# A new written order for the work of five engines in a fused scan and mixer kernel

## The chip, the cores and the metric

The kernel runs on one core of a Trainium2 chip. The metric is the time of one execution on the device in microseconds (us), lower is better. The engines are named as the profile names them: PE is TensorE's matmuls and PEld its weight loads, DVE is VectorE, ACT is ScalarE, POOL is GpSimd, SP is SyncE, which here only issues transfers (DMAs).

## The reference

Two blocks in a row. The first is a scan in the manner of Mamba 2 over 4 batches, 8 heads and 768 positions, with 32 channels and a state of 16, done in chunks of 32. The second is a mixer of low rank over the positions, followed by a two-layer network with residuals. The inputs are float32, but U, V and the two weights arrive as float64.

```python
def _attn_ref(x, a, B, C):            # x: (4, 8, 768, 32); a: (4, 8, 768); B, C: (4, 8, 768, 16)
    log_a = np.log(np.clip(a, 1e-06, 1.0))
    for c in range(S // 32):          # chunks of 32 positions
        cum = np.cumsum(la, axis=-1)  # la: log_a of the chunk
        L = np.exp(cum[:, :, :, None] - cum[:, :, None, :]) * causal
        M = np.einsum('bhin,bhjn->bhij', Cc, Bc) * L
        y_intra = np.einsum('bhij,bhjd->bhid', M, xc)
        y_inter = np.einsum('bhin,bhnd->bhid', Cc, state) * np.exp(cum)[:, :, :, None]
        y[:, :, sl] = y_intra + y_inter
        state = decay_full * state + sum_j(Bc * xc * decay_from_j)
...
    x = y as (4, 768, 256)            # positions by heads times channels
    u = x + (x^T @ U @ V)^T           # U: 768 x 32, V: 32 x 768
    out = u + max(u @ w_ch1, 0) @ w_ch2    # w_ch1: 256 x 1024, w_ch2: 1024 x 256
```

## The kernel before

The scan works on pairs of blocks of 128 positions: three pairs in a batch, twelve in all, numbered 0 to 11. The mixer works on a batch at a time: one projection to rank 32, one product back, then three blocks of 256 positions through the two-layer network. The weights arrive as pairs of 32-bit integers (the halves of float64) and are converted on the chip.

The order of all work is written out by hand in `PLANS` (lines 36 to 71) as a list of words, and `follow` executes them one after another. The scheduler is set to manual, so each engine gets its instructions in the order in which the words issue them. An engine never goes past an instruction that waits. A word may issue instructions on several engines, and a word that has several steps appears several times, one step at each appearance. The words that matter here:

- Loads, all on SP's one queue: `B` (B and C of a pair), `X` (x of a pair), `L` (both), `w0` and `w1` (halves of the first quarter of w_ch1, 256 KB each), `w2` to `w4` (its other quarters, 512 KB each), `w5` to `w8` (w_ch2), `Z1` (V) and `Z0` (U). Loads by `B`, `X`, `w` and `L` are held until the last VectorE instruction issued before them is done; `Z` is not.
- Conversion `c`: three steps, with two short VectorE operations and one of ScalarE (L420), one of ScalarE (L422), and three of VectorE. `c0` is U and V, `c1` and `c2` the halves of w1's first quarter, `c3` to `c5` its other quarters, `c6` to `c9` w2. `R` splits a converted quarter in two parts (three operations).
- The scan, with the pair's number behind it, counted from batch 1 (-3 to -1 is batch 0, 0 to 2 batch 1, 3 to 5 batch 2, 6 to 8 batch 3): `Q` or `P` scales B and C (VectorE); `V` or `T` turns them so that positions lie along the free axis (transposes on TensorE, L498, and copies on ScalarE); `D` or `E` decays B; `g` is the product of C and B (L584); `m` and `M` mask its two halves (VectorE); `s` and `u` compute and update the state (L619 on TensorE, then VectorE and POOL or ScalarE); `i` and `j` are the part of the output from the state (L714), `n` the part from within the chunk (L739); `y` copies the output to SBUF (L754 to L761, ScalarE). For the last three pairs `T` goes by four stores into DRAM and one fetch (L526, L532), and its last step scales what was fetched on ScalarE (L551, tile `Cm`).
- The mixer: `O` or `t` brings the output of a pair into another layout; `v` spreads U and V; `p` is the projection (L803) with its copy `pT` on ScalarE (L808); `x` is the product back (L815); `a` adds it to the scan's output (two VectorE operations each, tile `yT`); `U` is a product with w1 in plain float32 (L846) for batch 0's first two blocks; `S`, `f`, `e` and `h` are the same in three parts for all other blocks; `d` is a piece of the product with w2 (L846), whose last pieces add, transpose and store the result. The first number behind `p`, `x`, `a`, `S`, `f`, `e`, `h`, `d`, `U` says which batch: it is counted back from batch 1, so `U1` and `d1` are batch 0, `f0` is batch 1, `f-1` batch 2, `f-2` batch 3.

PSUM has three sets of banks, used in strict rotation: `w` with two, `x` with three, `z` with three. A group that asks for the next bank of a set waits until what was in it has been read.

The instructions of TensorE arrive in blocks of 16 KB by a transfer queue of their own (q8 in the profile): 25 packets in this execution for the whole program.

j-2, named in the prediction, has one small VectorE operation ahead of its products, a copy into the tile `settled`:

```python
    def inter(k, part):
        ...
        if part and "part" not in behind:
            apart(vector.tensor_copy)
        after = behind.pop("part", None)
```

`apart` issues that copy behind the products of the first part (for j-2 in the new order: of i-3), and the products of j wait for it.

Of the kernel before, what the change touches and what calls it, by code (L numbers as in the profile page):

```python
# [36 lines left out]
    0: (  # L37
        'B0 X0 B1 X1 B2 X2 '),
    1: (
        'Z1 F5 A0 Q-3.0 Q-3.1 A1 Q-3.2 F4 V-3.0.0 Q-2.1 V-3.1.5 K2 D-3 g-3 Q-2.2 Q-2.0 V-2.0.2 '  # L40
        'Z0 m-3 M-3 F2 V-2.1.2 Q-1.2 E-1.0 s-3 Q-1.0 D-2 n-3 w0 Q-1.1 V-1.0.2 u-3 F1 V-1.1.3 s-2 '
        'w1 i-3 g-2 u-2 j-3 y-3 F2 g-1 i-2 B3 B4 B5 w2 w3 X3 w4 X4 m-2 M-2 w5 c0 c0 m-1 B6 O-3.0 '
        'c0 M-1 w6 E-1.1 n-2 s-1 u-1 c2 v0 w7 c1 c2 j-2 i-1 y-2 j-1 n-1 c1 y-1 P0 D0 c1 T0 c2 '
        't-2 O-1.3 P2 X5 T0 X6 w8 P1 D2 p1.0.4 p1.4.6 c3 c3 x1 a1.0 a1.1 T1 T2 T2 T1 g0 U1.0.0 '
        'c3 c4 c4 U1.0.1 g1 m0 M0 c5 c4 m1 M1 c5 D1 s0 u0 U1.1.0 U1.1.1 U1.1.2 i0 n0 y0 c6 c6 s1 '
        'c5 g2 c7 u1 R2 m2 c7 U1.1.3 M2 c8 c8 c7 U1.0.2 L4 U1.0.3 i1 n1 y1 c6 R1 R0 c8 R5 c9 s2 '
        'c9 c9 n2 d1.0 L5 R6 u2 R0 d1.1 P3 S1.2 d1.0 R7 d1.0 i2 y2 R3 t1 R1 t0 R2 R5 d1.1 R4 P4 '
        'T3 d1.0 f1.2.0 R4 T4 f1.2.2 t2 e1.2.0 f1.2.1 R6 d1.0 d1.1 D3 R3 h1.2.0 P5 d1.1 e1.2.2 '
        'f1.2.3 e1.2.1 p0 T3 d1.2 e1.2.3 T4 T5 L6 h1.2.2 h1.2.1 R7 d1.1 x0 a0.0 a0.1 d1.2 h1.2.3 '
        'd1.2 d1.2 d1.2 s3 g3 m3 M3 d1.2 d1.2 S0.0 d1.2 g4 m4 M4 d1.2 d1.2 d1.2 d1.2 f0.0.0 '  # L50
        'f0.0.1 e0.0.0 T5 f0.0.2 f0.0.3 d1.2 D4 s4 e0.0.1 u3 e0.0.2 e0.0.3 L7 L8 D5 s5 h0.0.0 i3 '
        'n3 y3 d0.0 d0.0 u4 h0.0.1 g5 h0.0.2 u5 d0.0 d0.0 d0.0 h0.0.3 d0.0 m5 M5 d0.0 P6 d0.0 T6 '
        'n4 S0.1 i4 y4 d0.0 D6 d0.0 d0.0 d0.0 D8 f0.1.2 P7 T7 S0.2 f0.1.3 s6 n5 i5 y5 e0.1.2 '
        'e0.1.3 f0.2.0 u6 t5 h0.1.2 f0.1.0 f0.2.1 f0.2.2 e0.2.0 f0.2.3 e0.2.1 t3 f0.1.1 e0.2.2 '
        'e0.2.3 D7 t4 e0.1.0 h0.1.3 e0.1.1 d0.2 d0.2 d0.2 h0.2.0 h0.2.1 T6 d0.2 t3 h0.2.3 h0.1.0 '
        'd0.1 d0.2 h0.2.2 d0.1 d0.1 d0.1 d0.2 d0.2 d0.2 h0.1.1 d0.1 t4 T7 d0.0 P8 T8 s7 u7 g6 m6 '
        'd0.1 M6 t5 d0.1 d0.2 d0.1 d0.2 d0.2 d0.2 d0.1 d0.1 d0.1 d0.1 s8 u8 n6 i6 y6 p-1 g7 T8 '
        'd0.2 x-1 d0.1 m7 M7 n7 a-1.0 a-1.1 S-1.0 i7 y7 g8 f-1.0.2 f-1.0.3 m8 M8 n8 i8 y8 t6 t7 '
        'S-1.1 e-1.0.2 h-1.0.2 t6 e-1.0.3 f-1.0.0 f-1.0.1 h-1.0.3 t8 f-1.1.3 e-1.0.0 e-1.0.1 '
        'f-1.1.0 h-1.0.0 f-1.1.1 h-1.0.1 d-1.0 S-1.2 d-1.0 f-1.1.2 d-1.0 t7 e-1.1.0 h-1.1.0 '  # L60
        'e-1.1.1 e-1.1.2 e-1.1.3 d-1.1 d-1.0 d-1.0 h-1.1.1 d-1.0 d-1.1 d-1.0 d-1.0 h-1.1.2 d-1.1 '
        'd-1.1 t8 d-1.1 p-2 h-1.1.3 d-1.1 x-2 a-2.0 a-2.1 d-1.1 d-1.1 S-2.0 f-1.2.0 d-1.0 d-1.0 '
        'd-1.1 d-1.0 d-1.0 f-1.2.2 f-1.2.3 f-1.2.1 e-1.2.2 h-1.2.2 e-1.2.3 h-1.2.3 e-1.2.0 d-1.1 '
        'f-2.0.0 h-1.2.0 d-1.1 d-1.1 f-2.0.3 e-1.2.1 h-1.2.1 S-2.1 f-2.0.2 e-2.0.0 f-2.0.1 d-1.2 '
        'e-2.0.2 e-2.0.3 e-2.0.1 h-2.0.2 h-2.0.0 h-2.0.3 f-2.1.1 d-1.0 h-2.0.1 d-1.2 d-1.2 d-1.2 '
        'f-2.1.0 S-2.2 d-1.2 d-1.2 d-1.2 f-2.1.2 d-1.2 f-2.1.3 e-2.1.2 d-1.2 h-2.1.2 d-1.2 d-1.2 '
        'e-2.1.0 e-2.1.1 d-1.2 f-2.2.2 d-1.1 f-2.2.3 e-2.1.3 h-2.1.3 d-2.0 d-2.0 h-2.1.0 d-2.0 '
        'd-2.0 d-2.0 d-2.0 d-2.0 d-2.0 d-2.2 d-1.2 e-2.2.2 h-2.2.2 e-2.2.3 h-2.2.3 f-2.2.0 d-2.0 '
        'd-2.0 d-2.0 f-2.2.1 e-2.2.0 h-2.1.1 d-2.1 h-2.2.0 d-2.1 e-2.2.1 h-2.2.1 d-2.0 d-2.2 '
        'd-2.1 d-2.1 d-2.1 d-2.1 d-2.1 d-2.1 d-2.2 d-2.2 d-2.0 d-2.1 d-2.1 d-2.1 d-2.1 d-2.1 '  # L70
        'd-2.2 d-2.2 d-2.2 d-2.2 d-2.2 d-2.2 d-2.2 d-2.2 d-2.2 d-2.2 '),
}


# [1041 lines left out]
```

## Time and profile before

| what | number |
|---|---|
| time, median of three runs | 214.86 us (214.03 to 215.40) |
| profiled execution, span on the page (the only time that it gives) | 212.4 us |
| TensorE matmuls busy | 202.9 us, 96%, 3190 instructions |
| weight loads busy | 180.9 us, 85% |
| VectorE busy | 173.2 us, 82%, 363 instructions |
| ScalarE busy | 121.0 us, 57% |
| GpSimd busy | 6.3 us, 3% |
| SP's transfers | 20.95 MB, 53.9% of 16 DMA engines' span |
| first product with w1 (U1.0.0) starts | 33.84 us |
| last product with w2 ends | 208.6 us |

The page cuts the span into stretches in which an engine is busy or not; how long an engine stood idle, and what released it, stands in brackets behind a row of the timeline. Matmuls are pipelined, so a row of matmuls counts as busy also where it is not dense. The time of a run includes some us around the profiled span: the median here lies 2.5 us above the span of the one profiled execution.

### The profile page before, as it was taken

How to read it: one execution, taken by the hardware profiler on the slowest of the kernel's cores; microseconds unless marked ns; L12 is line 12 of the kernel's file. 1: busy time of each engine (PE TensorE's matmuls, PEld its weight loads, DVE VectorE, ACT ScalarE, POOL GpSimd, SP SyncE). 2: the span in 40 equal slices, each digit the busy share in tenths (PEclk: the TensorE clock that was granted, in tenths of full speed). 3: DMA queues.
4: the chain of work that ended last, by engine and by line, in shares of the span. 5: the costliest groups of instructions: out<-in, count | busy, mean ns of one | idle time of the engine just before them, and what ended most of it. 6: DMA issues, size and time to landing. Idle time of an engine off the chain costs nothing.

```text
span 212.4 us, 7511 instructions
## 1 busy us (share of the span) xinstructions
PE 202.9 (96%) x3190; PEld 180.9 (85%) x3190; DVE 173.2 (82%) x363; ACT 121.0 (57%) x279; POOL 6.3 (3%) x22
## 2 busy tenths in 40 slices
PE   7988889999999999999999999899999999999994
PEld 5765666878979997988999999589998999999993
DVE  4299979999899999999799995777986299859941
ACT  3354668489969746285588361669713565554310
POOL 4022000000000000000000000000000000000000
PEclk9999999999999999999999999999999999999999
DMA  5997799994751488356755766626510000324354
GB/s 82 138 150 160 89 246 181 190 241 121 102 71 31 79 207 130 88 83 83 108 89 94 149 143 132 112 38 122 117 52 0 0 5 0 49 32 71 49 102 99
DMA packets 120177, 21.43 MB, mean 101 GB/s; under 512 B 110096, under 2 KB 118352, under 8 KB 120144
## 3 DMA queue, kind: packets, MB, share of 16 engines
q1 hardware_dynamic: 120144, 20.95, 53.9%
q8 instruction: 25, 0.41, 0.9%
q14 instruction: 8, 0.07, 0.2%
HBM read 14.39 MB, written 6.55 MB: 99 GB/s over the span
## 4 chain that ended last, share of the span: by engine, by line
PE 75%; DVE 8%; issue 4%; DMA 4%; ACT 3%; SPq 3%; POOL 0%; POOLq 0%; DVEq 0%; ACTq 0%
PE x L846 35%; PE z L846 28%; DMA bc<-in_B_dram 4%; SPq L196 3%; DVE words L170 2%; PE x L584 2%; PE z L739 1%; PE w L803 1%; PE x L714 1%; PE x L739 1%; DVE S L170 1%; ACT yT L759 1%; PE x L815 1%; DVE o L170 1%; DVE BC L170 1%
## 5 line engine op out<-in xcount | busy, mean ns | idle before, releaser
L170 DVE SCALAR_TENSOR_TENSOR words<-words 128x512 fp32r<-128x512 f32 (+6 forms) x60 | 39.4, 669 | 2.4 <-ACT words L420 0.8
L846 PE MATMUL x<-words,w 128*128 128x256 f32 x288 | 38.1, 280 | 0.0
L846 PEld LDWEIGHTS x<-words,w 128*128 128x128 f32 x288 | 34.9, 188 | 1.6 <-issue 1.2
L846 PE MATMUL x<-u,w 128*128 128x256 f32 x240 | 34.3, 282 | 0.0
L846 PE MATMUL z<-u,w 128*128 128x256 f32 x240 | 32.7, 278 | 0.0
L851 ACT ACTIVATE x<-x 128x512 f32<-128x512 f32 (+1 forms) x27 | 15.5, 577 | 28.2 <-PE x L846 26.4
L846 PEld LDWEIGHTS x<-u,w 128*128 128x128 f32 x240 | 30.3, 188 | 0.6 <-ACT yT L759 0.2
L846 PEld LDWEIGHTS z<-u,w 128*128 128x128 f32 x240 | 29.7, 188 | 0.1
L851 ACT ACTIVATE z<-z 128x512 f32<-128x512 f32 (+1 forms) x24 | 13.7, 574 | 12.3 <-PE z L846 10.2
L846 PE MATMUL z<-words,w 128*128 128x256 f32 x144 | 19.6, 280 | 0.0
L846 PEld LDWEIGHTS z<-words,w 128*128 128x128 f32 x144 | 17.7, 188 | 0.9 <-issue 0.9
L170 DVE SCALAR_TENSOR_TENSOR words<-x,words 128x512 fp32r<-128x512 f32 x20 | 13.6, 682 | 4.5 <-ACT words L886 4.4
L170 DVE SCALAR_TENSOR_TENSOR words<-z,words 128x512 fp32r<-128x512 f32 x20 | 13.6, 682 | 2.2 <-ACT words L886 2.2
L886 ACT ACTIVATE words<-x 128x512 fp32r<-128x512 f32 x20 | 12.0, 598 | 3.3 <-PE x L846 3.2
L170 DVE TENSOR_TENSOR yT<-x,yT 128x384 f32<-128x384 f32 (+1 forms) x15 | 9.2, 613 | 5.1 <-PE x L846 2.7
L170 DVE TENSOR_TENSOR BC<-bc,F 128x512 f32<-128x512 f32 (+2 forms) x18 | 8.7, 508 | 5.4 <-DMA bc<-in_B_dram 3.0
L886 ACT ACTIVATE words<-z 128x512 fp32r<-128x512 f32 x20 | 11.8, 597 | 1.7 <-PE x L846 1.2
L170 DVE SCALAR_TENSOR_TENSOR S<-S,kept,w 128x64 f32<-128x64 f32 x40 | 11.2, 279 | 1.7
L584 PE MATMUL x<-Cm,T 32*64 32x128 f32 x192 | 11.6, 307 | 0.6 <-DVE Cm L170 0.4
L651 ACT ACTIVATE Sm<-S,slot 128x128 f32<-128x128 f32 (+1 forms) x18 | 6.0, 385 | 9.9 <-DVE S L170 9.9
L584 PE MATMUL z<-Cm,T 32*64 32x128 f32 x192 | 10.5, 307 | 0.0
L170 DVE TENSOR_TENSOR M<-x,causal 128x256 int32<-128x256 int32 x24 | 9.1, 421 | 1.6 <-PE z L584 1.6
(152 smaller groups left out, 363.5 us busy)
## 6 DMA issues: line engine op xcount, KB each, us to landing
words<-in_moe_w_ch_dram SPq DMA_DIRECT2D x7, 512.0 KB, 5.5
squares<-w1f SPq DMA_DIRECT2D x52, 64.0 KB, 1.9
x<-in_x_dram SPq DMA_DIRECT2D x24, 128.0 KB, 4.1
out_dram<-o SPq DMA_DIRECT2D x32, 64.0 KB, 2.3
bc<-in_B_dram SPq DMA_DIRECT2D x24, 64.0 KB, 3.5
bc<-in_C_dram SPq DMA_DIRECT2D x12, 128.0 KB, 3.9
T<-squares SPq DMA_DIRECT2D x6, 256.0 KB, 4.3
ytok<-squares SPq DMA_DIRECT2D x6, 256.0 KB, 3.6
```

What stands on the lines that cost most here:

```text
L170: self.last = call(*args, **kwargs)
L196: op = nc.sync.dma_start(**kwargs)
L584: nc.tensor.matmul(out=g[r][cols, c], lhsT=s["T"][rows, 0, c, cols], rhs=s["Cm"][rows, :, :, ts(2 * c + p, Q)].rearrange("r v t i -> r v i ...
L651: nc.scalar.activation(s["Sm"][:, sl, v], s["S"][:, sl, ts(v, D)], AF.Copy, scale=slot[:, v, None])
L714: product = nc.tensor.matmul(out=y[r // 2][p][ts(v, H), c], lhsT=own[ts(r, Q)], rhs=s["T"][ts(r, Q), 1, :, ts(2 * c + p, Q)].rearrange("r ...
L739: product = nc.tensor.matmul(out=y[n][p][ts(v, Q), c], lhsT=x_sb[k][half, c, h], rhs=s["M"][half, h // 2, c, h % 2], start=fresh(k, n, p, ...
L759: nc.scalar.copy(out=yp[ts(1 - v, H), n, :, p], in_=y[n][p][ts(v, H)])
L803: nc.tensor.matmul(out=p[ts(n, H)], lhsT=UU[:, c].rearrange("p t r -> p (t r)"), rhs=ytok[b][:, c, ts(n, P)], start=(c == 0), stop=(c == N ...
L815: nc.tensor.matmul(out=h[q][:, :VS], lhsT=pT[rows], rhs=V4[rows], start=True, stop=True, skip_group_check=True)
L846: nc.tensor.matmul(out=t, lhsT=lhsT, rhs=rhs, start=start, stop=True, skip_group_check=True)
L851: nc.scalar.activation(t, t, AF.Copy, scale=1.0 + EPS)
L886: nc.scalar.activation(gs[j, i][0], t, AF.Relu, scale=NEAR)
```

## The change

Only the second plan, `PLANS[1]`, changes (lines 40 to 71). It contains the same words, each as often as before (one `j-2`, three `c3`, and so on), in a new order; the fills `F` are the same. So each engine executes as many instructions of each kind as before. Below are the stretches of which the prediction speaks; the order between them is new as well.

```diff
-        'Z1 F5 A0 Q-3.0 Q-3.1 A1 Q-3.2 F4 V-3.0.0 Q-2.1 V-3.1.5 K2 D-3 g-3 Q-2.2 Q-2.0 V-2.0.2 '
-        'Z0 m-3 M-3 F2 V-2.1.2 Q-1.2 E-1.0 s-3 Q-1.0 D-2 n-3 w0 Q-1.1 V-1.0.2 u-3 F1 V-1.1.3 s-2 '
-        'w1 i-3 g-2 u-2 j-3 y-3 F2 g-1 i-2 B3 B4 B5 w2 w3 X3 w4 X4 m-2 M-2 w5 c0 c0 m-1 B6 O-3.0 '
-        'c0 M-1 w6 E-1.1 n-2 s-1 u-1 c2 v0 w7 c1 c2 j-2 i-1 y-2 j-1 n-1 c1 y-1 P0 D0 c1 T0 c2 '
-        't-2 O-1.3 P2 X5 T0 X6 w8 P1 D2 p1.0.4 p1.4.6 c3 c3 x1 a1.0 a1.1 T1 T2 T2 T1 g0 U1.0.0 '
-        'c3 c4 c4 U1.0.1 g1 m0 M0 c5 c4 m1 M1 c5 D1 s0 u0 U1.1.0 U1.1.1 U1.1.2 i0 n0 y0 c6 c6 s1 '
-        'c5 g2 c7 u1 R2 m2 c7 U1.1.3 M2 c8 c8 c7 U1.0.2 L4 U1.0.3 i1 n1 y1 c6 R1 R0 c8 R5 c9 s2 '
-        'c9 c9 n2 d1.0 L5 R6 u2 R0 d1.1 P3 S1.2 d1.0 R7 d1.0 i2 y2 R3 t1 R1 t0 R2 R5 d1.1 R4 P4 '
...
-        'n3 y3 d0.0 d0.0 u4 h0.0.1 g5 h0.0.2 u5 d0.0 d0.0 d0.0 h0.0.3 d0.0 m5 M5 d0.0 P6 d0.0 T6 '
-        'n4 S0.1 i4 y4 d0.0 D6 d0.0 d0.0 d0.0 D8 f0.1.2 P7 T7 S0.2 f0.1.3 s6 n5 i5 y5 e0.1.2 '
...
-        'd0.1 d0.2 h0.2.2 d0.1 d0.1 d0.1 d0.2 d0.2 d0.2 h0.1.1 d0.1 t4 T7 d0.0 P8 T8 s7 u7 g6 m6 '
-        'd0.1 M6 t5 d0.1 d0.2 d0.1 d0.2 d0.2 d0.2 d0.1 d0.1 d0.1 d0.1 s8 u8 n6 i6 y6 p-1 g7 T8 '
-        'd0.2 x-1 d0.1 m7 M7 n7 a-1.0 a-1.1 S-1.0 i7 y7 g8 f-1.0.2 f-1.0.3 m8 M8 n8 i8 y8 t6 t7 '
...
-        'd-1.1 t8 d-1.1 p-2 h-1.1.3 d-1.1 x-2 a-2.0 a-2.1 d-1.1 d-1.1 S-2.0 f-1.2.0 d-1.0 d-1.0 '
...
+        'F5 A0 A1 Q-3.0 Q-3.1 Q-3.2 F4 V-3.0.0 w0 V-3.1.5 Z1 K2 Z0 g-3 D-3 Q-2.1 s-3 Q-2.2 Q-2.0 m-3 '
+        'M-3 D-2 V-2.0.2 u-3 F2 V-2.1.2 Q-1.2 w3 w1 g-2 s-2 Q-1.0 Q-1.1 V-1.0.2 B4 m-2 u-2 c1 c1 F1 '
+        'V-1.1.3 w2 n-3 M-2 i-2 n-2 E-1.0 c1 i-3 j-2 c0 B3 j-3 c0 c0 E-1.1 c4 w7 X3 c2 s-1 y-3 y-2 '
+        'F2 g-1 u-1 w4 v0 c2 m-1 t-2 M-1 c4 B5 w6 i-1 O-3.0 j-1 P1 n-1 c4 p1.0.4 y-1 c3 O-1.3 c2 '
+        'p1.4.6 w5 c3 P0 T1 X4 x1 T1 a1.0 a1.1 c3 T0 D0 T0 U1.0.0 c8 c5 c5 U1.1.0 w8 B6 g0 m0 R1 c5 '
+        'R2 M0 s0 U1.1.1 c8 U1.1.2 u0 U1.0.1 c7 c8 X5 P2 U1.1.3 c6 g1 m1 c7 L4 c6 R3 U1.0.2 D1 M1 L5 '
+        'T2 T2 c6 U1.0.3 R6 c7 i0 n0 D3 s1 y0 R4 g2 X6 d1.0 u1 m2 d1.1 i1 n1 M2 c9 R5 D2 c9 c9 P4 s2 '
+        'L6 R0 u2 d1.1 d1.1 n2 i2 y1 d1.0 R1 P3 y2 R0 T3 R2 T4 d1.0 S1.2 t0 f1.2.2 R6 f1.2.1 f1.2.0 '
...
+        'T6 D7 n3 y3 d0.0 d0.0 d0.0 d0.0 n4 i4 y4 u5 L8 d0.0 d0.0 g5 m5 S0.2 d0.0 d0.0 f0.1.0 f0.1.1 '
+        'e0.1.0 M5 n5 s6 i5 P7 y5 e0.1.1 T7 f0.1.2 h0.1.0 t5 t3 f0.2.0 e0.1.2 f0.1.3 h0.1.1 f0.2.1 '
...
+        's7 t4 m6 d0.0 d0.2 d0.2 D8 d0.1 d0.1 M6 d0.2 d0.1 u7 g7 s8 u8 d0.1 d0.2 d0.2 d0.2 m7 M7 T8 '
+        'd0.1 d0.2 n6 p-1 d0.2 i6 x-1 a-1.0 n7 i7 a-1.1 y6 S-1.0 g8 y7 t6 f-1.0.2 f-1.0.1 m8 M8 t7 '
...
+        'h-1.1.1 d-1.0 d-1.0 d-1.0 t8 p-2 d-1.0 x-2 h-1.1.0 a-2.0 d-1.0 d-1.0 S-1.2 d-1.0 f-1.2.0 '
...
```

What can be read from it in words: the first half of w1 is loaded ahead of V and U, and the conversion of that half (`c1`) comes ahead of that of U and V (`c0`). The gram and state products of the first pairs follow one another more closely. `i-3` comes behind `n-2`, and `j-2` ahead of `j-3`. All three steps of `c4` and the first of `c3` come ahead of `O-1.3`, which feeds the last projection of batch 0. `P2`, `T2` and `g0` come behind the first products with w1, and these go through the second block (`U1.1.0`) before the second quarter of w1 (`U1.0.1`). Near the start of batch 2's mixer, `p-1` stands ahead of `i6` and `y6` instead of behind them, `g7` stands far ahead of `n6`, and the last step of `T8` (Cm on ScalarE) stands ahead of `p-1`. `p-2` has a piece of a down product between it and `x-2`.

36 rows, old and new, of the table PLANS are left out of this document.

## The prediction

> **What bounds the kernel now.** I read the busy shares first, then busy time by stage, then the timelines where TensorE (PE) is not full.
>
> ```profile
> PE 202.9 (96%) x3190; PEld 180.9 (85%) x3190; DVE 173.2 (82%) x363; ACT 121.0 (57%) x279; POOL 6.3 (3%) x22
> ...
> q8 instruction: 25, 0.41, 0.9%
> ```
>
> TensorE is busy for 202.9 of 212.4 us and the change takes no instruction away, so only its 9.5 us of gaps, the part of the start in which matmuls wait while counted as busy, and the tail can change. By stage (length, then busy us and instructions of PE, weight loads, DVE, ACT and POOL, granted clock, DMA share, GB/s):
>
> ```profile
> 0.00:34.00 34.00, 29.22 (x627) 21.63 (x628) 24.92 (x79) 18.16 (x48) 6.27 (x22) 1.00 0.86 147
> 34.00:60.00 26.00, 25.37 (x486) 20.64 (x487) 24.34 (x58) 19.25 (x44) 0.00 (x0) 1.00 0.74 155
> 60.00:100.00 40.00, 39.78 (x564) 35.22 (x564) 38.90 (x76) 26.84 (x62) 0.00 (x0) 1.00 0.59 101
> ...
> 130.00:140.00 10.00, 9.29 (x313) 6.78 (x313) 8.09 (x19) 5.39 (x18) 0.00 (x0) 1.00 0.60 116
> 140.00:160.00 20.00, 20.00 (x269) 19.16 (x267) 15.64 (x28) 11.93 (x26) 0.00 (x0) 1.00 0.38 81
> 160.00:200.00 40.00, 40.00 (x354) 39.45 (x354) 30.39 (x49) 20.79 (x38) 0.00 (x0) 1.00 0.17 27
> ```
>
> The clock is 1.00 throughout, so it is no term. From 140 to 200 TensorE is gapless: a delay put in before 140 reaches the end in full unless a later wait absorbs it. From 34 to 100 VectorE (DVE) is nearly as full (63.2 of 66 us), so what is moved on it shifts all behind it. The places that can move are the start up to the first up product (U1.0.0, 33.84), the waits of 34 to 60, two spots near 96, and 130 to 140.
>
> **The change part by part.** Every engine has the same instructions; only their order differs. The sum starts from the profiled execution's span, 212.4; the page gives no other time of its own, and the median, 214.86, lies 2.5 above the span. I add the 2.5 at the end.
>
> *Loads.* The 256 KB half of w1 that comes first goes ahead of V and U on SP, whose earlier loads are issued back to back until 13.05. Such a load landed 4.6 us after its issue, so 17.7; its conversion c1 now stands where VectorE arrives at about 17.8. The other weight loads also come before their conversions, with 512 KB landing after 5.5. Value 0, between 0 and 0.8 (if the 5.5 holds for the first half too).
>
> *Instruction blocks.* TensorE stops inside a word where nothing releases it:
>
> ```profile
> 20.87 0.18 PEld L739 LDWEIGHTS x<-M,x 64*32 64x32 f32 x6
> 21.60 0.10 PEld L739 LDWEIGHTS x<-M,x 64*32 64x32 f32 x1 [0.55 <-issue]
> ```
>
> Stops fall at every 256th PE instruction where the 256 before were short ones: 0.38 lost at 16.78, 0.66 at 21.60, 0.38 at 25.53, 0.43 at 96.42 (inside n3): 1.9 in all. The new order gives n3's block 5.1 us of dense work ahead of its end instead of 3.1, which ends that stop, and leaves 3.24 us in the block that ends in i4, which should start one. Value 0; between -1.9 (all stops gone) and +1.5 (three more like the mean). The Trainium skill, page "Runtime: NRT & Kernel Launch", section "Instruction fetch mechanics", says that the sequencer fetches the next block of 256 instructions while it executes the current one, and calls a crossing mostly hidden. By that the four stops would be near zero before and after, and the term 0 with no chance of -1.9; the 0.55 above is against it for short instructions, while the stretch 140 to 200 is for it.
>
> *The start, on VectorE.* The rows:
>
> ```profile
> 29.84 1.29 DVE L170 TENSOR_TENSOR BC<-bc,F 128x512 f32<-128x512 f32 x2 [1.36 <-DMA bc<-in_B_dram]
> ...
> 32.06 0.55 DVE L170 TENSOR_TENSOR yT<-x,yT 128x384 f32<-128x384 f32 x1
> ...
> 33.45 0.55 DVE L170 TENSOR_TENSOR yT<-z,yT 128x384 f32<-128x384 f32 x1
> ```
>
> The yT rows are a1.0 and a1.1; a1.0 releases U1.0.0. Adding the rows of every word ahead of a1.0, VectorE has 26.76 us of work before it now and 28.10 then: +1.34 (c4's first and last steps, 0.88 and 2.14, come forward; D0 0.42, D2 0.42, P2 0.69 and small others go back). P2's wait of 1.36 leaves the path, because P2 moves behind U1.1.2: -1.36. Q-2.1 no longer fills the wait at 9.95: +0.3. The new wait is j-2's small copy (0.14), which must follow TensorE's i-3, itself now behind n-2 and M-2; queued behind it on VectorE are c0, c4, u-1, m-1 and M-1, and so n-1, y-1, the last projection of batch 0 and x1. The nearest row is the same copy for j-3, which waited nothing at 17.40; the other bound is i-3 plus its dependants, 1.5. In the new order M-2 comes right ahead of n-2, n-2 and i-3 last 0.9 and 0.5 on TensorE, and VectorE has c1's last step of 1.26 in between, which covers a part: I take +0.85, nearer to the second row. Sum +1.13, so a1.0 starts at 33.2 at the overlap that VectorE's rows show now, and at 33.9 if the moved work runs without it; 33.5 taken. a1.0's two operations last 1.02: U1.0.0 at 34.55, +0.7 (0.4 to 1.1).
>
> *TensorE's work ahead of U1.0.0.*
>
> ```profile
> 31.19 1.09 PE L498 MATMUL w<-ident,BC 128*128 128x128 f32 x8 [0.22 <-DVE BC L170]
> ...
> 33.84 1.99 PE L846 MATMUL x<-yT,w1f 128*128 128x256 f32 x8
> ```
>
> Now the turns of pair 2 (two, 0.49 each) and g0 (0.86) run while TensorE would wait for a1.0; in the new order both come behind U1.0.0, so the cover is gone and 1.84 us more work lies behind it: +1.84. If they fitted later gaps it would be 0; by 60 only 1.6 us of gaps are there, below. Together with the start: +2.5.
>
> *34 to 60.* A late TensorE finds some results ready. U1.0.1 lost 0.42 waiting for c3; c3's last step is 1.34 us of VectorE work later, but U1.1.0, 1.8 us, now stands ahead of U1.0.1. The plain down product lost 0.6 (0.43 to 0.75) waiting for c9; VectorE's work ahead of c9's last step is 54.59 against 54.33, so it is as early as it was. Both go: -1.0. The 0.6 near 46.6, for y0's copies ahead of the next x and z banks, stays: g2 and d1.0 now stand behind y0. +1.5 by 60.
>
> *60 to 130.* x0's two groups follow M3 more closely: +0.2. n3's saved 0.43 is in the block term, and 0.7 more is saved where i3, s5 and d0.0 waited; against that g5 waits for banks that y4 empties, with two down products (0.9) over y4's copies of 0.27 (+0.4), and n5, e0.1.2 and f0.2.0 stand closer to M5 and y5 (+0.7): net +0.4, between -0.7 (cover holds everywhere) and +1.4 (no cover for y4).
>
> *130 to 140.* ScalarE is in the way now:
>
> ```profile
> 133.13 0.27 ACT L761 COPY yT<-x 128x128 f32<-128x128 f32 x1 [0.63 <-DVE o L170]
> ...
> 134.68 0.27 ACT L808 COPY pT<-w 128x128 f32<-128x128 f32 x1
> 135.31 0.91 ACT L551 ACTIVATE Cm<-T,slot 128x256 f32<-128x256 f32 x2 [0.36 <-DMA T<-squares]
> ```
>
> pT stands behind y6's six copies, and x-1 follows at 135.00; TensorE lost 2.3 us from 130 to 142. Afterwards pT comes ahead of y6, and g7 is earlier (-2.3), but n6 now waits for the banks that M7 reads (one mask step, 0.7), x-1 (0.3), n7 (0.4) and g8 (0.6) for copies and masks put closer to them: +2.0; net -0.3. p-2 gets a down product behind it that hides its copy: -0.3 of 0.45. The tail is left as it is: the last product ends 3.8 before the end in both, as its chain (add, transpose, four stores) is the same.
>
> The sum: 0 + 0 + 0.7 + 1.84 - 1.0 + 0.2 + 0.4 - 0.3 - 0.3 = +1.5; 213.9 of span, and with 2.5, 216.4.
>
> **The rivals.**
> *Slower, by the Cm of pair 8 on ScalarE (L551).* In the new order its two operations, which wait for a fetch by DMA, stand ahead of pT's copy (now they are behind it). Behind them on ScalarE wait pT, then y6, y7 and the scalings of the first products; x-1, a-1.0 and S-1.0 wait for pT, and all of batch 2's mixer for those. A fetch landed 4.3 us after its issue (131.02 to 135.3). SP's queue puts it behind t4's fetch and the four stores of a finished block (4.8 us for seven such issues now), so it can be issued near 130 at the earliest: landing 134.3, Cm done 135.2, as pT is wanted at about 135. From an issue at 131 on, each us goes to the end in full. At 133, where SP's stores stood in the profile (132.47), it is +2, and with 0.7 for TensorE's next bank +2.7: 216.4 + 2.7 = 219.1. For it: L551 waited for that DMA (0.36) even now, with six copies ahead of it. Against: 130 would be on time.
> *Faster, because the early delay is not handed on.* j-2 finds i-3 done (-0.85), the two turns and g0 fit gaps that I counted as lost (-1.84), and the block stops go (-1.9); the two waits of 34 to 60 then come back in full (+1.0): 213.9 - 3.6 = 210.3 of span, 212.8; with the -0.7 bound of 60 to 130 in place of +0.4, 211.7. Centre 212.3. For it: P2's 1.36 is really removed, and no other wait at the start is longer but that of Q-2.1. Against: VectorE has 1.34 us more ahead of a1.0.
> *No effect.* The start is late by 1 to 2 us and the waits at 46.6, 96 and 135 absorb it, as they are waits for engines that did not get later: 214.9.
>
> **How the numbers follow.** My forecast has 0.36, the slower rival 0.26, the faster 0.28, no effect 0.10. The time is the likeliest's, 216.4. One per cent, 2.15 us, is about what can be told from no change here: faster is below 212.7, slower above 217.0. Of the faster rival's cases, 211.7 to 212.8 and up, 0.20 of its 0.28 lie below 212.7. Slower takes the 0.26 and 0.11 of my forecast, the cases with the loads' 0.8 or the blocks' +1.5: 0.37. Within 1%: 0.43. The range goes from 211.7, the faster rival's low end, to 220.0, the slower rival with one more us of late fetch; the forecast alone is 214.8 (j-2's wait and the +0.7 of 60 to 130 gone) to 218.7 (loads and blocks at their upper ends).
>
> **What would show it right or wrong.** Right: U1.0.0 starts at 34.3 to 35.2, with one turn of pair 2 and L584's g0 behind it; DVE shows a wait ahead of the settled copy and none for in_B_dram near 30; TensorE shows no idle time for w1f or o words in 34 to 60; an issue stop moves from 96 to the block in i4; ScalarE's pT row lies ahead of yT's in the stretch near 135. The slower rival shows as L551 waiting over 1 us for T right ahead of L808. Wrong: U1.0.0 before 33.8, no stops at all in the early blocks, or a gap of over 1 us in 140 to 200, of which I foresee none.

## The result: 1.2% slower

The changed kernel takes 217.92 us (median of seven runs, 216.91 to 219.23) against 215.65 (214.03 to 216.17): a ratio of 1.0123, 95% interval 1.0085 to 1.0161. On a second chip the unedited new order came to 1.0181 (1.0124 to 1.0237). Its profiled execution spans 215.1 us, of a run of 217.2, beside the 212.4 of the profile before. The forecast was 216.4. The direction was right; several of its terms were not.

First the page of the changed kernel: busy time, and the granted clock in 40 slices of 5.4 us.

```profile
PE 204.1 (95%) x3190; PEld 181.3 (84%) x3190; DVE 173.1 (80%) x363; ACT 122.7 (57%) x279; POOL 6.3 (3%) x22
...
PEclk9997589999999999999999999999999999999999
```

Then the same stretches as before (length, busy us of PE, weight loads, DVE, ACT, POOL, clock, DMA share, GB/s):

```profile
0.00:34.00 34.00, 26.83 (x566) 19.51 (x566) 22.39 (x72) 15.46 (x41) 6.34 (x22) 0.85 0.91 161
34.00:60.00 26.00, 25.93 (x397) 20.44 (x404) 25.35 (x61) 21.51 (x47) 0.00 (x0) 1.00 0.78 139
60.00:100.00 40.00, 40.00 (x625) 36.02 (x630) 37.44 (x72) 25.74 (x60) 0.00 (x0) 1.00 0.42 81
...
130.00:140.00 10.00, 10.00 (x302) 8.21 (x300) 7.51 (x20) 5.19 (x15) 0.00 (x0) 1.00 0.52 101
140.00:160.00 20.00, 19.66 (x284) 17.73 (x283) 16.18 (x30) 13.11 (x31) 0.00 (x0) 1.00 0.47 93
160.00:200.00 40.00, 40.00 (x352) 39.83 (x351) 28.49 (x46) 20.98 (x37) 0.00 (x0) 1.00 0.19 34
```

The start is where it differs: 61 TensorE instructions fewer by 34 us, VectorE busy 2.5 us less (22.39 against 24.92), and a clock of 0.85 where before had 1.00. From 34 to 60 TensorE is fuller than before. So VectorE did not have too much to do at the start, as the prediction had it: it waited.

VectorE's timeline of the changed kernel shows for what:

```profile
18.37 0.56 DVE L169 TENSOR_SCALAR words<-words 128x256 int32<-128x256 int32 x2 [1.20 <-DMA words<-in_moe_w_ch_dram]
18.86 0.59 DVE L169 TENSOR_SCALAR Cm<-x,slot 128x128 f32<-128x128 f32 x2
19.38 0.74 DVE L169 TENSOR_TENSOR M<-z,causal 128x256 int32<-128x256 int32 x2
...
22.40 0.15 DVE L169 COPY settled<-slot 128x1 f32<-128x1 f32 x1 [1.16 <-PE z L713]
...
33.87 0.42 DVE L169 COPY ytok<-z 128x256 f32<-128x256 f32 x1 [1.33 <-PE z L768]
```

The first row is c1, waiting for w0. It was issued at 14.25, not at 13.05, and landed 4.1 us later. Behind it on VectorE stand V-1.1.3's copy (Cm) and the mask M-2, and TensorE's i-2 needs a bank that M-2 reads:

```profile
17.11 0.35 PE L713 MATMUL x<-T,Sm 32*64 32x64 f32 x4
19.93 0.37 PE L713 MATMUL z<-T,Sm 32*64 32x64 f32 x2 [2.46 <-DVE M L169]
```

From there to x1 the chain that ended last in the changed kernel runs nearly without a break through TensorE's short words, and then through ScalarE. A part of it (start, us, what):

```profile
24.50 1.15 PE x L139 x2
...
27.56 0.74 PE z L1011 x8
28.30 0.52 ACT V L1015 x2
28.82 0.41 ACT words L421
29.23 0.55 ACT ytok L782
29.78 0.62 ACT words L421
30.40 0.48 ACT ytok L782
30.88 0.04 issue
30.93 0.28 PE z L713 x2
```

L139 is the idle fill F2 ahead of g-1, L1011 is v0. The last L782 is O-3.0's copy, for which j-1's products wait (the role that a `settled` copy has elsewhere): on ScalarE it stands behind v0's two copies, c2, t-2 and c4. So x1 starts at 35.15 instead of 30.04 and U1.0.0 at 36.72 instead of 33.84.

How much of that reaches the end is read from TensorE's lateness: the start of a word less the unhindered lengths of all TensorE words ahead of it in that kernel's own order (0.91 for an f, 0.45 for an e or d, 0.25 for a T, which is two transposes, and so on, as they last in the dense stretches of before; where words run a little shorter than that, it falls). From the two profiles:

| at | before | after | difference |
|---|---|---|---|
| x1 | 4.02 | 9.38 | +5.4 |
| U1.0.0 (after: T2 and g0 still to come) | 5.12 | 9.35 | +4.2 |
| d1.0 | 5.14 | 8.73 | +3.6 |
| x0 | 3.58 | 6.73 | +3.2 |
| s8 | 6.49 | 9.25 | +2.8 |
| f-1.0.2 | 8.46 | 10.55 | +2.1 |
| last product | 9.79 | 12.54 | +2.75 |

The two spans differ by 2.7: the account closes. The start loses 5.4, later stages give back 3.3 of it (their waits are for engines that did not get later), and the tail loses 0.7.

One execution is not a rule, though. Three executions with before's start had U1.0.0 at 33.84, 34.20 and 35.32; three with the new start at 36.72, 36.79 and 38.26. The shown profile of before is the earliest of its kind, and the difference of the means is 2.8. It is also the only one of the fourteen profiles in which the granted clock stays at 1.00 from the start to the end of the products. So the table is the account of this pair, not of every pair.

### The profile page after: what moved, and what is told of

It is laid out like the page before. It is cut to its first block, busy times and chain, and to the rows that moved or that the text cites. A ratio compares the mean times of both kernels' runs of the same rounds, so it can differ in the third digit from the quotient of the medians.

```text
span 215.1 us, 7532 instructions
## 1 busy us (share of the span) xinstructions
PE 204.1 (95%) x3190; PEld 181.3 (84%) x3190; DVE 173.1 (80%) x363; ACT 122.7 (57%) x279; POOL 6.3 (3%) x22
## 4 chain that ended last, share of the span: by engine, by line
PE 86%; SPq 6%; ACT 3%; DMA 2%; DVE 1%; issue 1%; ACTq 0%
PE x L845 37%; PE z L845 28%; SPq L195 6%; PE x L583 3%; PE x L738 2%; PE w L802 2%; PE z L738 2%; DMA words<-in_moe_w_ch_dram 2%; PE w L618 2%; PE z L713 2%; PE x L713 2%; PE x L814 2%; PE x L802 1%; PE w L497 1%; PE z L583 1%
## 5 line engine op out<-in xcount | busy, mean ns | idle before, releaser
L845 PE MATMUL x<-words,w 128*128 128x256 f32 x288 | 40.7, 282 | 0.0
L845 PEld LDWEIGHTS x<-words,w 128*128 128x128 f32 x288 | 35.9, 188 | 1.9 <-issue 1.4
L845 PE MATMUL x<-u,w 128*128 128x256 f32 x240 | 33.8, 281 | 0.5 <-ACT x L850 0.5
L845 PE MATMUL z<-u,w 128*128 128x256 f32 x240 | 33.1, 278 | 0.0
L845 PEld LDWEIGHTS x<-u,w 128*128 128x128 f32 x240 | 30.0, 188 | 1.3 <-ACT x L850 0.9
L845 PEld LDWEIGHTS z<-u,w 128*128 128x128 f32 x240 | 29.8, 188 | 0.2
L845 PE MATMUL z<-words,w 128*128 128x256 f32 x144 | 19.9, 277 | 0.0
L845 PEld LDWEIGHTS z<-words,w 128*128 128x128 f32 x144 | 17.9, 188 | 0.1
L713 PE MATMUL z<-T,Sm 32*64 32x64 f32 x180 | 8.5, 254 | 3.5 <-DVE M L169 2.5
L583 PE MATMUL x<-Cm,T 32*64 32x128 f32 x192 | 10.5, 317 | 1.4 <-ACT Cm L507 1.0
L169 DVE TENSOR_TENSOR BC<-bc,F 128x512 f32<-128x512 f32 (+2 forms) x18 | 9.2, 531 | 1.7 <-ACT F L371 1.5
L169 DVE TENSOR_TENSOR u<-yT,u 128x512 fp32r<-128x512 f32 x10 | 6.9, 687 | 4.3 <-ACT u L839 4.3
L583 PEld LDWEIGHTS x<-Cm,T 32*64 32x64 f32 x192 | 6.6, 138 | 4.2 <-ACT Cm L507 1.2
```

Of the source, the lines that this page charges most:

```text
L169: self.last = call(*args, **kwargs)
L583: nc.tensor.matmul(out=g[r][cols, c], lhsT=s["T"][rows, 0, c, cols], rhs=s["Cm"][rows, :, :, ts(2 * c + p, Q)].rearrange("r v t i -> r v i ...
L713: product = nc.tensor.matmul(out=y[r // 2][p][ts(v, H), c], lhsT=own[ts(r, Q)], rhs=s["T"][ts(r, Q), 1, :, ts(2 * c + p, Q)].rearrange("r ...
L845: nc.tensor.matmul(out=t, lhsT=lhsT, rhs=rhs, start=start, stop=True, skip_group_check=True)
```

## The experiments

All are edits of the written order. Ratios are to before on the same chip. One row each, with U1.0.0 from its profile:

| run | U1.0.0, us | ratio (95% interval) |
|---|---|---|
| changed kernel | 36.72 | 1.0123 (1.0085 to 1.0161) |
| after_again | 38.26 | 1.0181 (1.0124 to 1.0237) |
| m2_before_c1 | 36.02 | 1.0115 (1.0052 to 1.0178) |
| fill_the_gap | 36.99 | 1.0092 (1.0058 to 1.0126) |
| ytok_early | 36.60 | 1.0058 (1.0019 to 1.0098) |
| m2_and_ytok | 37.45 | 1.0051 (1.0008 to 1.0094) |
| m2_and_no_fill | 34.78 | 1.0095 (1.0063 to 1.0127) |
| after_to_85_then_before | 36.79 | 1.0069 (1.0031 to 1.0108) |
| before_to_85_then_after | 34.20 | 1.0068 (1.0025 to 1.0111) |
| before_to_88_then_after | 35.32 | 1.0060 (1.0018 to 1.0101) |
| before_to_25_then_after | 42.24 | 1.0336 (1.0275 to 1.0396) |
| before_t2_g0_late | 34.28 | 0.9964 (0.9924 to 1.0004) |
| before_no_fill | 34.69 | 0.9947 (0.9908 to 0.9986) |

**The wait for w0.**

```diff
- m-2 u-2 c1 c1 F1 V-1.1.3 w2 n-3 M-2 i-2
+ m-2 u-2 F1 V-1.1.3 w2 n-3 M-2 c1 c1 i-2
```

> The changed kernel, with the first two steps of c1 moved behind M-2, so that the mask M-2 and V-1.1.3's copy no longer stand on VectorE behind the wait for w0's load. Theory W (the start is late because of this one wait: VectorE idle 1.20 us, TensorE idle 2.6 us, and then a granted clock of 0.5 from 18.7 to 28.6 us): the clock is 1.00 throughout, TensorE's gap before i-2 is under 0.5 us, U1.0.0 starts at 34 to 35 instead of 36.72, and the time is 2 to 3 us under the changed kernel, 215.0 to 216.0. Rival V (VectorE's order decides: it has more work ahead of a1.0, and the wait only hides that): U1.0.0 at 36 or later, time within 0.7 us of the changed kernel, 217.2 to 218.6.

The gap ahead of i-2 shrank as meant (from 2.46 to 0.71 us), and n-2 started 1.2 us sooner (19.36 instead of 20.55), but U1.0.0 only 0.7, and the ratio did not move. The granted clock fell all the same, to 0.5 from 18.3 to 28.6. The weight loads of this run show that other waits remained:

```profile
18.71 0.21 PEld L713 LDWEIGHTS z<-T,Sm 32*64 32x64 f32 x2 [0.83 <-POOL Sm L646]
...
22.06 0.18 PEld L713 LDWEIGHTS z<-T,Sm 32*64 32x64 f32 x2 [0.33 <-issue]
...
30.22 0.14 PEld L713 LDWEIGHTS z<-T,Sm 32*64 32x64 f32 x2 [0.93 <-ACT ytok L782]
```

The stop at 22.06, inside j-2, comes 1.3 us after a packet of instructions had landed (19.80 to 20.76), and j-1 still waits for O-3.0's copy. Theory W, that the one wait makes the loss, is refuted: neither its clock nor its start nor its time came. The wait is one link; the 0.7 us are less than the 1.5 by which two executions of the unedited order differ (the control, below). Rival V's numbers all but came (36.02; 218.63), but its reason is not shown by that: what j-1 waits for here is ScalarE.

**The clock.** In the new order it is at half for 10.2 us, as the stretches show (columns as above):

```profile
16.00:18.00 2.00, 1.46 (x72) 1.05 (x70) 1.00 (x4) 0.30 (x2) 0.75 (x2) 1.00 0.95 252
18.00:20.00 2.00, 0.07 (x4) 0.10 (x6) 1.63 (x6) 1.36 (x4) 0.58 (x2) 0.67 0.99 326
20.00:22.00 2.00, 2.00 (x86) 1.71 (x88) 1.20 (x4) 0.37 (x1) 0.00 (x0) 0.50 1.04 198
22.00:28.00 6.00, 5.74 (x114) 3.54 (x106) 5.04 (x17) 2.98 (x8) 0.51 (x1) 0.50 0.74 137
28.00:30.00 2.00, 2.00 (x28) 1.48 (x24) 1.67 (x4) 1.72 (x5) 0.00 (x0) 0.77 0.88 170
```

Two runs ask what that costs. One fills the gap:

```diff
- V-1.1.3 w2 n-3 M-2 i-2 n-2
+ V-1.1.3 w2 n-3 M-2 F6 i-2 n-2
```

> The changed kernel, with three more idle products of TensorE (F6: about 2.1 us of work whose results nobody reads) put in front of i-2, into the gap in which TensorE waits for M-2; the wait itself stays. It parts the clock from the wait. Theory W1 (a gap of over 1.3 us costs the clock, and the clock at half is a cost of its own): the granted clock stays 1.00 in 18 to 29 us, i-2 still starts near 19.9, U1.0.0 comes 1 to 2 us sooner than 36.72, and the time is 216.2 to 217.2. Rival W2 (the clock at half lies under VectorE's work and costs nothing): clock 1.00, but U1.0.0 at 36.5 or later and a time of 217.5 to 218.3.

The clock stayed at 1.00 until 22, then fell for two windows anyway, and U1.0.0 did not come sooner (36.99). So neither theory's condition, a clock of 1.00 to 29 us, was met, and the run does not part them. At 23.16 this run has a stop of 0.87 for instructions, 1.3 us after a packet that landed at 21.83. The other run takes the fills out of before, which leaves TensorE less busy:

```diff
- F2 V-2.1.2    F1 V-1.1.3    F2 g-1
+ V-2.1.2       V-1.1.3       g-1
```

> The kernel before without its three idle fills F2, F1 and F2 (TensorE products that nobody reads, some 0.7, 0.4 and 0.7 us, ahead of V-2.1.2, V-1.1.3 and g-1). It asks what the clock is worth at the start in an order that has no wait for w0. Theory C (half clock on a chain of TensorE's own work costs time): the granted clock falls to 0.5 in one to three windows of 3.4 us between 15 and 29, U1.0.0 comes 0.5 to 2 us later, the ratio 1.003 to 1.010. Rival W2 (half clock lies under VectorE's work): the clock falls, U1.0.0 stays within 0.4 us and the ratio within 0.997 to 1.003.

```profile
14.00:18.00 4.00, 2.25 (x85) 1.50 (x74) 3.54 (x13) 1.93 (x7) 1.20 (x2) 1.00 0.89 199
18.00:22.00 4.00, 3.82 (x97) 3.33 (x97) 2.82 (x11) 1.71 (x4) 0.97 (x2) 0.56 0.68 124
22.00:26.00 4.00, 4.00 (x128) 2.89 (x127) 3.64 (x11) 1.59 (x5) 0.51 (x1) 0.59 0.82 93
```

The clock fell to half here as well, and the kernel got faster: 215.24 against 216.68 us, ratio 0.9947 (0.9908 to 0.9986). Theory C's ratio is refuted for the old order, and W2 falls short on the good side: the fills cost more than what they keep. That rests on the ratio alone: U1.0.0, at 34.69, came 0.85 later than in the profile of before, which is C's number, though inside the scatter of the old start (33.84 to 35.32), and this profile has a stop for instructions of 1.59 us at 48.72 that the one of before has not. By the ratio this version beats both kernels.

What half clock costs in the new order, whose chain runs through TensorE's own words from 20 to 28, stays open: in no run was the clock full with all else alike. The executions of before beside these experiments give a hint for the old order (79 of them, each against the mean on its own chip). With a clock of 1.00 over the whole execution (34 of them) they took 0.27 us less than that mean; with about 0.99, which is one window of 3.4 us at half (37), 0.16 more; with less (8), 0.40 more. So one window goes with 0.4 us, give or take 0.2; whether it is the cause is not shown. The changed kernel's executions list 0.974 to 0.984, two or three windows; if each cost as much there, an estimate from these numbers, some 1 us of the 2.65 would be the clock's.

**ScalarE's queue ahead of j-1.**

```diff
- y-2 F2 g-1 ... i-1 O-3.0 j-1
+ y-2 O-3.0 F2 g-1 ... i-1 j-1
```

> The changed kernel with O-3.0 (the turned output of pair 0, whose copy on ScalarE the products of j-1 wait for) moved from behind i-1 to ahead of g-1; j-1 then waits for a small VectorE copy behind i-1 instead. Theory S (the start is late because j-1 waits on ScalarE, whose queue holds v0's two copies, c2, t-2's copy and c4 ahead of O-3.0's copy: chain 26.74 to 30.93 in the new profile): j-1 starts at 29.6 to 29.9 instead of 30.93, U1.0.0 at 35.4 to 36.0 instead of 36.72, and the time is about 1 us under the changed kernel, if later waits do not take it back. Rival C (the granted clock of 0.5 from 18.7 to 28.6 us decides the start): U1.0.0 stays at 36.4 or later.

j-1 started at 30.65 instead of 30.93, and U1.0.0 at 36.60. The edit put in a wait of its own, since O-3.0 needs y-3's copies, and g-1 now queues behind it:

```profile
24.82 0.72 PEld L768 LDWEIGHTS x<-ident,yT 128*128 128x128 f32 x4 [0.69 <-ACT yT L753]
```

Theory S's numbers did not come. Rival C's did (36.4 or later), but the new wait ahead of g-1 would give the same, so the clock is not shown to be the cause. The ratio, 1.0058, is below the 1.0181 of the same kernel unedited, measured on another chip; nothing in its profile explains that, so it isn't counted as a gain.

With both edits together:

> Both edits of the start: c1 behind M-2, and O-3.0 ahead of g-1. Theory S with the wait for w0 as its first half: M-2's 1.2 us are no longer swallowed by ScalarE's queue, so j-1 starts at 28.5 to 29.0, U1.0.0 at 34.2 to 35.2, the time 215.0 to 216.5 beside a before of 215.5 to 217, about level with it. Rival C: clock 0.5 in two or three windows of 3.4 us from 18 us on, U1.0.0 at 35.8 or later, a time above before's by 1% as the changed kernel's.

n-2 was the earliest yet (19.05), and j-2 then stopped for 1.58 us inside itself:

```profile
22.63 0.14 PEld L713 LDWEIGHTS z<-T,Sm 32*64 32x64 f32 x2 [1.58 <-issue]
```

The packet with those instructions landed at 21.37. Theory S's numbers did not come (j-1 at 31.49); U1.0.0, at 37.45, is where rival C had it, its 1% is not: what the two edits gained was lost to the block of instructions and to O-3.0's wait. The ratio of 1.0051 with such a profile again can't be put down to a cause.

**Taking work off the chain.** m2_before_c1's edit, and the new order's three fills left out:

> The changed kernel with c1 behind M-2, and without the three idle fills F2, F1 and F2 ahead of V-2.1.2, V-1.1.3 and g-1. In the new profile the last fill lies on the chain (24.50 to 25.65, 1.15 us at half clock), between s-1 and g-1, where nothing waits on VectorE. Theory K (the start of the new order is one chain through TensorE, M-2's wait and then the queue of short words behind it, so that each piece taken off it shows): x1 at 32.8 to 34.0 instead of 35.15 (36.69 in the second profile), U1.0.0 at 34.4 to 35.6, the ratio to before 1.002 to 1.010 against 1.012 and 1.018 of the unedited order. Rival B (the blocks of instructions and ScalarE's copies end at the same time as the chain, so that nothing shows): x1 at 34.5 or later, the ratio above 1.010, as in m2_before_c1.

x1 at 33.22 and U1.0.0 at 34.78 are where theory K put them, and the last product ends earliest of all runs with the new start; the ratio, 1.0095, is at the upper edge of K's range. This was the only edit of the new start that moved U1.0.0 by more than 1 us from the first profile's 36.72. It is one execution, though, and the fastest of its eleven (216.01, with a median of 217.80); the ratio hardly differs from that of m2_before_c1 (1.0115). So theory K fits the profile, and a gain in time is not shown. What is left of the waits in it:

```profile
22.41 0.18 PEld L713 LDWEIGHTS x<-T,Sm 32*64 32x64 f32 x2 [1.17 <-issue]
...
28.99 0.13 PEld L713 LDWEIGHTS z<-T,Sm 32*64 32x64 f32 x2 [1.31 <-ACT ytok L782]
```

**Pair 2's turn (T2, T2) and g0 by themselves.** The prediction's largest term, put into before:

```diff
- x1 a1.0 a1.1 T1 T2 T2 T1 g0 U1.0.0 c3
+ x1 a1.0 a1.1 T1 T1 U1.0.0 T2 T2 g0 c3
```

> The kernel before with one edit: the turns of pair 2 and g0 come right behind U1.0.0 instead of ahead of it. This is the prediction's +1.84 by itself. By the prediction: U1.0.0 starts up to 0.7 us sooner, 1.84 us of TensorE's work comes later, so +1.1 us at U1.0.1 less what its wait for c3 (0.42) gives back: +0.7 at 41 us, and +0.5 to +1.1 at the end. Rival: TensorE only waits less further on, and the time is within 0.3 us of before's.

0.9964 (0.9924 to 1.0004): no loss, against the +0.5 to +1.1 us of the prediction. U1.0.0, with less ahead of it, waits for a1.0 instead, and U1.0.1's wait for c3 is still there, at 37.60:

```profile
34.28 0.30 PEld L845 LDWEIGHTS x<-yT,w1f 128*128 128x128 f32 x2 [1.06 <-DVE yT L169]
...
37.60 1.59 PEld L845 LDWEIGHTS z<-yT,w1f 128*128 128x128 f32 x8 [0.43 <-DVE w1f L169]
```

It is the ratio that says so. The one profile, with a span of 214.8, can't be set beside that of before: x1 came 1.1 us later (31.12), ahead of the edit, and at a block of instructions at 49.40 TensorE stopped for 1.53 us, which it did not in before.

**Which half loses.** Splices: one order up to a word, then all that is left in the other's order.

> The new order up to a0.1 of batch 1 (some 85 us), and behind it the old order of all that is left. Theory W: the loss of the start stays in full to the end: 3.15 us more lateness at x0 than before, less nothing: 218.0 to 219.0. Rival A (later waits of the old order, at 96, 131 to 142, absorb a part, since they are waits for engines that did not get later): 216.3 to 217.5.

> The order of before up to a0.1 of batch 1 (some 80 us), and behind it the new order of all that is left. Theory W: all the loss lies in the start, and the rest of the new order is level with the old or up to 0.5 us better (TensorE's lateness grows by 5.8 us from x0 to the end in the new profile and by 6.2 in the old): 214.7 to 215.9, beside before's 215.65. Rival T (T8's scaling on ScalarE, which stands ahead of pT's copy, is hidden in the new profile only because TensorE is 3 us late there): pT waits for the fetch, and the time is 216.5 to 218.

The new start with the old rest is slower by 0.69% (0.31 to 1.08), with lateness 6.79 at x0 and 13.03 at the end: 6.2 from x0 on, as in before. So in the profile the old rest absorbs nothing, as theory W has it. The ratio asks for less than W's 3.15 us: 1.5, between 0.7 and 2.3, which is rival A's size. The median, 218.56, is where W put it only because before itself took 217.17 on this chip and W had reckoned from 215.65. W's 3.15 rests on the early profile of before, so the two are not parted. The old start with the new rest is slower too (0.68%), where its theory W had it level. Its seam has a part in it: g4 follows d1.2 at once there and waits 0.42 for M3. So the seam was moved:

> As the earlier splice, with the seam at M4 (some 88 us) instead of a0.1, so that g4, m4 and M4 stand as in before and no product has to wait at the seam. Theory (all the loss lies ahead of x0): a ratio of 0.996 to 1.003. Rival (the new order behind 88 us loses as well, when TensorE comes to it in time, by T8's scaling ahead of pT or by closer copies near 108 to 142): 1.004 to 1.010.

1.0060 (1.0018 to 1.0101): where TensorE comes to it in time, the new order behind 88 us loses as well. By the ratios the two halves lose about alike, 0.69% and 0.60%, together about the 1.23% of the whole; the pair of profiles above, which puts more than the whole ahead of x0, is not the rule. But the second half does not lose by the cause that rival T gave. Its ScalarE:

```profile
134.25 0.91 ACT L550 ACTIVATE Cm<-T,slot 128x256 f32<-128x256 f32 x2 [1.15 <-DMA T<-squares]
136.22 0.27 ACT L807 COPY pT<-w 128x128 f32<-128x128 f32 x1 [1.06 <-PE w L802]
```

Cm does stand ahead of pT's copy and waits 1.15 us for its fetch, yet pT then waits another 1.06 for TensorE's p-1. From f-1.0.2 to the last product, lateness grows by 2.7 us in this run, by 2.0 in the changed kernel and by 1.3 in before: in this profile the loss lies behind 140 us. One place of it shows in the changed kernel too: e-1.0.0, with a single f between it and its own f-1.0.0, waits for the scaling on ScalarE.

```profile
147.25 0.53 PEld L845 LDWEIGHTS x<-u,w 128*128 128x128 f32 x4 [0.44 <-ACT x L850]
```

Half of the 1.4 us, some 0.7, is not the order's: from 160.8 to 174.8 and from 197.9 to 205.9 us the products of this execution start 117.8 ns apart, where those of before and of the changed kernel start every 113.3, with a granted clock of 1.00 in all three. Whether its other executions have such stretches is not recorded, so the ratio of 1.0060 may contain them. The rest is spread in pieces of under 0.25 and was not traced.

**A splice that failed.**

> The order of before up to j-1 (some 25 us), and behind it the new order of all that is left, seam unsmoothed. Theory S (what is lost is lost before n-1, from the wait for w0's load and from ScalarE's queue): n-1 starts at 26 to 27.5, U1.0.0 at 32.5 to 34.5, and the time is within 1 us of before's. Rival V (VectorE's extra work ahead of a1.0 is the loss, as the prediction had it): U1.0.0 at 35 or later though n-1 is early.

n-1 came at 27.5, as theory S said, and then VectorE stood still:

```profile
33.71 0.76 DVE L169 TENSOR_SCALAR words<-words 128x512 int32<-128x512 int32 x2 [5.62 <-DMA words<-in_moe_w_ch_dram]
```

The new order converts the third quarter (c4) first, the old order issues its load only at 27.96. It tells nothing between S and V; it shows what a conversion ahead of its load costs: 5.6 us of VectorE's wait, 8 us at U1.0.0.

**The control.**

> The changed kernel itself, unedited, beside before on the chip of this comparison, so that the other edits can be read against it. If the start is set by the same chain each time, its profile has n-1 at 31 to 32 and U1.0.0 at 36 to 37 again, with the granted clock at 0.5 in two to three windows of 3.4 us between 18 and 29 us; the ratio to before 1.005 to 1.016.

n-1 at 32.90, 0.9 us past the range, U1.0.0 at 38.26, 1.3 us past it, and a ratio of 1.0181, past it as well; half clock from 20 on; M-2's gap is again there (2.44 us). The start's lateness varies by 1.5 us between executions and is carried to the end: 10.92 at x1 and 14.58 at the last product. Of the 1.5, 1.23 are a stop for instructions inside j-2, 1.4 us after a packet that landed at 23.10; the first profile has none there:

```profile
24.46 0.18 PEld L713 LDWEIGHTS z<-T,Sm 32*64 32x64 f32 x2 [1.23 <-issue]
```

## Why the prediction was right or wrong

- *The sum* (+1.5) had the sign, and the time is in the range: the ratio makes it 2.65 (1.23% of 215.65), the medians differ by 2.27. That it came so near is luck: a term of +1.84 that is nothing stood in for the 2.2 us by which the start was missed (U1.0.0 at 36.72, not 34.55).
- *Loads, 0 (0 to 0.8): failed.* c1's wait was foreseen at nothing and was 1.20 us: the two x loads ahead of w0 on SP took 2.98 us to issue instead of 1.88, and VectorE was at c1 by 17.2, not 17.8. The price is not the 1.2 but what stands behind c1: the step named no one, and it was M-2 and with it TensorE, 2.46. Taking that wait away alone (m2_before_c1) did not change the time.
- *The start on VectorE, +0.7 (0.4 to 1.1): mis-sized.* U1.0.0 came 2.9 later (2.8 between means). j-2's wait was sized nearly rightly (1.16 for 0.85). What the step left out was the other two engines: TensorE's queue of short words behind M-2, and j-1's wait on ScalarE. By 33.87 VectorE waits for TensorE (1.33), not the other way round.
- *T2 and g0, +1.84: failed, and misread.* The eight transposes in the row at 31.19 are two turns of 0.49, pair 1's and pair 2's, and only pair 2's moves: by its own rows the term was 0.49 + 0.86 = 1.35. By the ratio the move costs nothing (0.9964).
- *34 to 60, -1.0: right in kind, smaller.* Lateness falls by 0.6 from U1.0.0 to d1.0, in before by nothing; U1.0.1 and the down product no longer wait for c3 and c9.
- *60 to 130, +0.4: wrong sign, small.* From x0 to s8 the new order gains 0.4. *130 to 140, -0.3: right way, -0.7.* *p-2, -0.3: not seen*; from f-1.0.2 on the new order loses 0.7. *The tail, as it was: right.* The last product ends 3.2 us before the end in both (at 209.24 and 211.99); the 208.6 and the 3.8 given ahead are those of the start of the last word.
- *Clock "no term": failed as a statement*, half clock for 10.2 us; that it cost time was not shown, only that executions of before with a window of it took some 0.4 us longer.
- *Blocks, 0: right in the first pair of profiles* (n3's stop is gone, one of 0.27 in i4 is there), and wrong in what it left out: the block that ends inside j-2, at 22 to 24.5. The first profile has no stop there, the second of the same order 1.23, the new start with the old rest 1.28, and the edits of the start 0.33 to 1.58 where they have one. So it is no limit that an edit exposes, but one that some executions meet. What the Trainium skill says (page "Runtime: NRT & Kernel Launch", section "Instruction fetch mechanics"), that a crossing is mostly hidden, holds in these traces where words are long: behind 162 us no end of a block shows a stop in either profile of the pair.
- *Slower rival (Cm ahead of pT): its sign came, its cost did not.* L550 waited 1.84 us for a fetch issued at 132.57, right ahead of pT's copy, as the rival had it. But Cm was done at 136.41, and pT then waited another 0.36 for p-1, since TensorE was late itself. *Faster rival:* no. The 0.28 for it rested on T2 and g0 fitting gaps, which they do, and on j-2, which waited.

## What to carry to other kernels

An operation that waits for a transfer is priced by the queue behind it, not by its own wait: name the next mask or copy on that engine, and who needs it. Where several waits end within a us of each other (here a load, a block of instructions, another engine's queue), removing one shows the next; only with work taken off the chain as well did U1.0.0 move by more than two executions differ, and that in one execution. Ask of idle fills what they hide: leaving three of them out of the old order gained 0.5% (0.1 to 0.9), although the clock then fell. And read one profile as one execution: here starts differ by 1.5 us, and tails by up to 2, with the order unchanged or the edit far ahead of them.

## What the runs showed of the hardware

- The granted clock moves in windows of about 3.4 us: half for 3.4 us (19.1 to 22.5 in before_to_85_then_after), 6.8 (21.0 to 27.8 in after_to_85_then_before), 10.2 (18.7 to 28.9 in the changed kernel). No length of gap decides it: in the changed kernel it fell at 18.69, 1.2 us into the gap of 2.46; in m2_before_c1 it fell at 18.3, with no idle stretch of TensorE over 0.9 us in the 3.4 us before, and for as long; in before_to_88_then_after it fell at 27.7 with none over 0.3. A stretch of 1.7 us between 8.2 and 11.6 in before_no_fill did not lower it. What decides is not shown. The Trainium skill, page "TensorE: Matmul & The Clock Gate", section "HAM oscillation — how this bites in real kernels", gives the rule as no idle gaps over about 3.4 us; here the rule is too mild: the clock fell after the much shorter ones just named.
- A packet of TensorE's instructions took about 1 us, and the instructions could run about 1.3 us after it landed (20.76 to 22.06, 21.37 to 22.63, 21.83 to 23.16, 23.10 to 24.46).
- TensorE has two paces that the granted clock does not tell apart. Its products of 128x256 (L845, L846 in before) start 113.3 ns apart in most dense stretches and 117.8 in others, with a clock of 1.00 in both. Behind f-1.0.2 the slower pace holds for 21 of 556 products in the changed kernel (0.1 us lost), for 208 in before_to_88_then_after (0.9), 267 in m2_before_c1 (1.2) and 457 in fill_the_gap (from 161.9 us to the end, 2.0). What sets it is not shown.
